# Two pieces of the column transform's last form in places of sums, and raw chunks of the hidden DFT matrices behind the forms' stores

## The chip, the cores and the metric

The kernel runs on one core of a Trainium2 chip, as one program with one launch. The metric is the device time of one execution in microseconds, the median over a few executions. A profiled execution gives a trace of every engine: PE (TensorE matmuls), PEld (its weight loads), DVE (VectorE), ACT (ScalarE), POOL (GpSimd) and SP (SyncE, which here only issues DMAs, in program order).

## What is computed

The reference takes x of 2048 rows by 640 columns and adds three things: x itself, the real part of a two-dimensional DFT of the normalised x, and a dense layer pair with GELU.

```python
xn = layernorm(x)                                # rows of 640
a = einsum("bsd,ed->bse", xn, dft_hid_re)        # wr in the kernel
b = einsum("bsd,ed->bse", xn, dft_hid_im)        # wi
y = einsum("ts,bse->bte", dft_seq_re, a) - einsum("ts,bse->bte", dft_seq_im, b)
out = x + y + (gelu(xn @ w1 + b1) @ w2 + b2)
```

All matrices are float32 and come as inputs; S is 2048, D is 640 and the hidden width F is 1536.

## The kernel before

Every product is made of three matmuls: each float32 operand is split into a high and a low part (`split`: a copy on ACT, line 157, then a subtraction on DVE, line 158), and `product` (lines 269 to 271) or `hidden` (line 287) adds high by high, high by low and low by high. One matmul is 128x128 by 128x512.

**First half: the dense layers.** Rows go through in four tiles t of 512 rows. Each has 12 steps i, one for each 128 hidden columns. In a step the program writes down `background` (loading, statistics and normalising for the next tile, ACT's square root among them), then `hidden(g + 2)` (15 matmuls), its `gelu` (line 296 on ACT, the split at 300 and 302), then `output(g)` (15 matmuls) with the `hs` of two steps before, and last, in the steps that `w_steps` lists, one step of `prep_w`. At t and step 9 the operand `XT` of the next tile is built (`prep_xt`, after `transpose_z` from `z`), and at step 10 the first `hidden` of the next tile reads it.

**The raw chunks.** `prep_w` turns wr and wi into seven matrices, kept in DRAM as `wit0` to `wit6`, for the second half's column transform. It goes over five chunks j of 128 rows, three steps k each. At k = 0 the raw chunk (`wraw0`, `wraw1`, one buffer each) is turned on DVE (`turn_w`, line 345) into `wt0` and `wt1`; before the change the next raw chunk is then asked for (`load_w`, line 340, 8 DMAs in pieces of 128 bytes). The steps then make two, two and three splits into a staging tile `wst` with two buffers, and each is stored by SP (`put_w`, line 361). A third `wst` cannot be written before the store of the first has landed. All these DMAs go through SP's one queue with the normalised rows (`xs`, line 200), `z` (line 226) and the loads of x (line 175).

**Second half: the two transforms.** The sequence transform runs in eight stages "s", one for each pair (h, t) in `blocks`; its sums u, u1, u2, v, v1, v2 lie in tiles of the pool `fr`, of which there are two sets (tags such as `u1_0` and `u1_1`). After blocks 5 and 7 follows a stage "y", the column transform of two row tiles, which the code calls hidden, too (`hidden_beside`, `hidden_entry`). A stage "y" has seven forms w of three entries each, 21 entries n. Form w multiplies sums by the five pieces of `wit[w]`, whose order is c = 0, 2, 1, 3, 4 and whose places in that order are called pos 0 to 4; piece number i is 5w + pos. `load_g(b, i)` asks for a piece. In the first stage "y" (b = 5, the one the change touches) there are five places, three in the tile `ws` and two in `gr_b`, used in turn; after each entry `hidden_entry` asks for the piece that goes into the place just read. The last form, w = 6, is 45 matmuls: its first entry (n = 18) uses pos 0 to 3 for the odd columns and pos 0 and 1 for the even ones, n = 19 uses pos 2 and 3, n = 20 uses pos 4. Of its pieces, number 30 is asked for at n = 13 and lies in a tile of its own, `gr`, that takes the place of the sum u2 of set 1; the other four use the five places.

Between the entries `hidden_beside` writes down other work of stage "y": `load_yb` reads the rows `ys` made in the first half into the places of u1 and u2 of set 0 (line 1057, runs of 256 bytes), `in_two` adds to them and stores them as output (line 803), and `load_part` reads the sums of the next block (line 786).

Of the kernel before, what the change touches and what calls it, by code (L numbers as in the profile page):

```python
# [11 lines left out]
F32R = mybir.dt.float32r  # L12
# [3 lines left out]
P = 128  # L16
Q = 4
B = 32
# [7 lines left out]
def kernel(  # L26
# [47 lines left out]
    ND = D // P  # L74
# [288 lines left out]
    def prep_w(s):  # L363

        j, k = divmod(s, 3)
        if j >= ND:
            return
        if k == 0:
            turn_w(0, j)
            turn_w(1, j)  # L370
            if j + 1 < ND:
                load_w(0, j + 1)
                load_w(1, j + 1)
        (r1, r2, r4), (i1, i2, i4) = (
            (A["wt", m][:, : 2 * P], A["wt", m][:, 2 * P : 4 * P], A["wt", m][:, 4 * P :]) for m in range(2)
        )

        if k == 0:
            put_w(0, j, r1, r4)
            put_w(1, j, i1, i4)  # L380
            add(r4, r4, i4)
        if k == 1:
            put_w(6, j, i2, i4, True)
            add(i2, i2, r2)
            put_w(2, j, i2, r4)
            add(r2, r1, r2, ALU.subtract)
            add(r1, i2, r1, ALU.subtract)
            add(i1, i1, r1, ALU.subtract)
        if k == 2:
            put_w(3, j, r1)  # L390
            put_w(4, j, i1)
            put_w(5, j, r2)

    def add(dst, a, b, op=ALU.add):
        nc.vector.tensor_tensor(dst, a, b, op=op)
# [71 lines left out]
    NW = 7  # L467
# [238 lines left out]
            form(2)  # L706


    w_steps = [(1, i) for i in (1, 2, 3, 5, 6, 7, 8)] + [(2, i) for i in (0, 1, 2, 3, 5, 6, 7, 8)]
    gelu(0, acc0)  # L710
    gelu(1, acc1)
    for g in range(NG):
        t, i = divmod(g, NF)
        if t == 0:
            prep_w1(i + 3)
            prep_w2(i + 1)
            load_w1(i + 6)
            load_w2(i + 4)
        background(t, i)
        if i == 10 and t + 1 < NT:  # L720
            load_xo(t)
        if i == NF - 1:
            acc = hidden(g + 2) if g + 2 < NG else None
            output(g)
            if acc is None:

                fourier_step(i)
                break

            def fill(k):  # L730
                for e in ((0,), (1, 2))[k]:
                    add_block(xo[t], e, oacc[t][e], f"ot{t}_{e}", bias=b2c[:, e : e + 1])

            gelu(g + 2, acc, fill)
            for e in (3, 4):
                add_block(xo[t], e, oacc[t][e], f"ot{t}_{e}", bias=b2c[:, e : e + 1])
            nc.sync.dma_start(ys[t], xo[t])
        elif i == NF - 2:
            output(g)
            if g + 2 < NG:  # L740
                gelu(g + 2, hidden(g + 2))
        else:
            acc = hidden(g + 2)
            if i == NF - 3 and t + 1 < NT:
                for j in range(ND):
                    prep_xt(t + 1, j)
                    if j + 2 < ND:
                        transpose_z(t + 1, j + 2)
            gelu(g + 2, acc)
            output(g)  # L750
        if t == 3 and i < NF - 1:
            fourier_step(i)
        if (t, i) in w_steps:
            prep_w(w_steps.index((t, i)))


    es_rows.close()
# [13 lines left out]
    def fr_tile(shape, tag, name, dtype=F32):  # L771
        return fr.tile(list(shape), dtype, tag=tag, bufs=1, name=name)
# [242 lines left out]
    def load_g(b, i):  # L1015
        if i >= NW * ND:
            return
        w, c = G[i]
        n = GWIDE[w] * P
        places = A["g", b]  # L1020
        k = i % len(places)
        if b < len(blocks) - 1 and w == NW - 1:

            k = (i - 1) % len(places)
            if c == 0:
                places, k = [fr_tile((P, 6 * P), f"u2_{sets[blocks[b]]}", f"gr_{b}", F32R)], 0
        g = places[k][:, : 2 * n].rearrange("p (a b) -> p a b", a=2)
        GT[b, i] = g
        nc.sync.dma_start(g.bitcast(F32), wits[w][c])

    def hidden_beside(b, n):


        ta, tb = blocks[b - 1][1], blocks[b][1]
        last = b == len(blocks) - 1
        x_, y_, z_ = (banks[:, k : k + 2] for k in (X, Y, Z))
        us, vs = bank(US), bank(VS)
        ya = yo[ta]

        def s(which, k):  # L1040
            return sums[(ta, tb)[which], k]

        def t2(k):
            return lambda: add(s(1, KU[k]), s(1, KV[k]), s(1, KU[k]), ALU.subtract)

        def t3(k):
            return lambda: add(s(0, KU[k]), s(1, KU[k]), s(0, KU[k]), ALU.subtract)

        def t4(k):
            return lambda: add(s(0, KV[k]), s(0, KV[k]), s(1, KU[k]), ALU.subtract)  # L1050

        def columns(k):

            return s(1 if last else 0, ("u1", "u2")[k]).rearrange("p a b -> p (a b)").rearrange("p (n e) -> p n e", n=NB)

        def load_yb(k):
            return lambda: nc.sync.dma_start(columns(k), ys[tb][:, :, 2 * k * B : 2 * (k + 1) * B])

        def copy(dst, src):
            return lambda: nc.scalar.activation(dst, src, AF.Copy)  # L1060

        def to(dst, acc, name, then=lambda: None):


            def f():
                add_turned(dst, turned(acc, name))
                then()

            return f

        def out_a(c0, c1):
            return lambda: store(ta, ya[:, :, c0:c1], c0, c1) if last else None

        def odd():
            yt = turned(us, f"yo_{tb}")
            add_turned(ya[:, :, 4 * B :], yt)
            add_turned(yo[tb, 4], yt)
            out_a(4 * B, DQ)()

        def in_two(k):  # L1080

            acc, name = s(1, ("v2", "v1")[k]), f"yb{k}_{tb}"

            def f():
                if name not in A:
                    A[name] = turned(acc, name)
                else:
                    add_turned(columns(k), A.pop(name))
                    store(tb, columns(k), 2 * k * B, 2 * (k + 1) * B, last and k == 1)

            return f

        yb1, yb2 = in_two(0), in_two(1)
        yb4 = to(yo[tb, 4], vs, f"yb4_{tb}", lambda: store(tb, yo[tb, 4], 4 * B, DQ, last))
        f5s = [lambda u=u: f5(u) for u in range(2)] if not last else [lambda: None] * 2
        f6s = [lambda u=u: f6(u) for u in range(2)] if not last else [lambda: None] * 2
        pre = {
            17: [lambda: add(s(1, "v1"), s(1, "v1"), x_)],
        }.get(n, [])
        post = {  # L1100

            0: [lambda: gather(1, tb, "v1", z_), lambda: gather(1, tb, "v", vs, op=ALU.subtract), f5s[0]],
            1: [f5s[1]],
            3: [to(ya[:, :, : 2 * B], x_, f"ya1_{ta}")],
            4: [t2(0)],
            5: [t2(1)],
            6: [to(ya[:, :, : 2 * B], y_, f"ya2_{ta}", out_a(0, 2 * B)), t2(2)],
            7: [odd],
            8: [t3(0)],
            9: [copy(s(1, "v1"), z_), t3(1)],  # L1110
            10: [t3(2)],
            11: [t4(0)],
            12: [copy(s(1, "v2"), x_), t4(1)],
            13: [load_yb(0), t4(2)],
            14: [load_yb(1), lambda: add(s(1, "v2"), s(1, "v2"), z_), yb1],
            15: [yb1],
            17: [yb2, yb2] if last else [],
            18: [yb4] if last else [yb2],
            19: [] if last else [yb2, f6s[0]],
            20: [] if last else [f6s[1], yb4],  # L1120
        }.get(n, [])
        if not last:
            if n == 13:
                post.append(lambda: load_g(b, (NW - 1) * ND))
            if n == 15:
                post.append(lambda: load_part(blocks[b + 1][1], "u1"))
            if n == 18:
                post.append(lambda: load_part(blocks[b + 1][1], "u"))
            if n == 20:
                post.append(lambda: load_a(put_off[0]))  # L1130

                def end():
                    to(ya[:, :, 2 * B : 4 * B], x_, f"ya3_{ta}")()
                    store(ta, ya, 0, DQ)

                later.append(end)
        return pre, post
# [19 lines left out]
    def hidden_entry(n, b, w, u):  # L1157
# [36 lines left out]
        for pos in mine:  # L1194
            i = w * ND + pos + len(A["g", b])
            if last or i < (NW - 1) * ND:
                load_g(b, i)
            elif i < NW * ND - 1:
                load_g(b, i + 1)

    first = 0
    for kind, what in stages:
# [67 lines left out]
```

## Time and profile before

| | us |
|---|---|
| median of 3 runs | 878.21 |
| lowest and highest | 877.09, 879.48 |
| profiled execution, its own time | 876.56 |
| span of that execution's trace | 874.8 |
| PE busy in it | 856.1 (98%) |
| DVE busy | 622.4 (71%) |
| ACT busy | 333.0 (38%) |

Times in the trace count from the start of its span; 1.76 us of the execution's time lie around the span. In a timeline a row gives start, duration, engine, line, operation, output and inputs, a count where equal ones are merged, and in brackets the idle time before it with what ended it. Matmuls overlap, so that a PE that runs without a gap starts one every 0.227 us though each is drawn 0.39 us long. A row with "SPq" is the time in which SP's queue took one DMA instruction; when the data is there is told by another view, "us to landing".

### The profile page before, as it was taken

How to read it: one execution, taken by the hardware profiler on the slowest of the kernel's cores; microseconds unless marked ns; L12 is line 12 of the kernel's file. 1: busy time of each engine (PE TensorE's matmuls, PEld its weight loads, DVE VectorE, ACT ScalarE, POOL GpSimd, SP SyncE). 2: the span in 40 equal slices, each digit the busy share in tenths (PEclk: the TensorE clock that was granted, in tenths of full speed). 3: DMA queues.
4: the chain of work that ended last, by engine and by line, in shares of the span. 5: the costliest groups of instructions: out<-in, count | busy, mean ns of one | idle time of the engine just before them, and what ended most of it. 6: DMA issues, size and time to landing. Idle time of an engine off the chain costs nothing.

```text
span 874.8 us, 10224 instructions
## 1 busy us (share of the span) xinstructions
PE 856.1 (98%) x3754; PEld 704.4 (81%) x3754; DVE 622.4 (71%) x792; ACT 333.0 (38%) x460; POOL 21.0 (2%) x22
## 2 busy tenths in 40 slices
PE   8999999999999999999999999999999699999997
PEld 6888888778888888888888888888888588888885
DVE  6554543465273678989988887889968679886586
ACT  5454433353253555434434343232323223223241
POOL 0000300030003000000000000000000000000000
PEclk9999999999999999999999999999999899999999
DMA  6746376666636984948743679574855939904465
GB/s 182 228 128 171 76 205 148 187 149 202 163 138 170 324 354 93 226 98 200 178 132 98 167 226 285 139 167 102 196 173 172 261 91 234 318 19 174 121 167 104
DMA packets 196017, 152.34 MB, mean 174 GB/s; under 512 B 70016, under 2 KB 170624, under 8 KB 194944
## 3 DMA queue, kind: packets, MB, share of 16 engines
q1 hardware_dynamic: 190016, 149.73, 63.6%
q10 hardware_dynamic: 5952, 1.97, 0.9%
q8 instruction: 29, 0.48, 0.2%
q14 instruction: 20, 0.16, 0.1%
HBM read 108.67 MB, written 42.99 MB: 173 GB/s over the span
## 4 chain that ended last, share of the span: by engine, by line
PE 87%; DVE 4%; DMA 3%; SPq 3%; ACT 1%; POOL 1%; issue 1%; DVEq 0%; ACTq 0%; POOLq 0%
PE banks L269 24%; PE banks L270 24%; PE banks L271 24%; PE banks L287 15%; DMA wit<-wst 2%; SPq L340 2%; SPq L200 1%; POOL xo L328 1%; DMA ws<-wit 1%; DVE wst L158 1%; DVE st L182 0%; DMA x<-in_A_x_dram 0%; DMA wraw<-in_A_dft_hid_im_dram 0%; DVE as L158 0%; ACT wst L157 0%
## 5 line engine op out<-in xcount | busy, mean ns | idle before, releaser
L270 PE MATMUL banks<-as,xab 128*128 128x512 f32 x407 | 158.5, 389 | 0.0
L271 PE MATMUL banks<-as,xab 128*128 128x512 f32 x407 | 158.4, 389 | 0.0
L269 PE MATMUL banks<-as,xab 128*128 128x512 f32 x407 | 158.3, 389 | 0.0
L157 ACT ACTIVATE as<-r 128x1024 fp32r<-128x1024 f32 x80 | 85.0, 1062 | 182.9 <-PE banks L271 162.2
L158 DVE TENSOR_TENSOR as<-r,as 128x1024 fp32r<-128x1024 f32 x80 | 97.1, 1215 | 49.7 <-ACT as L157 49.7
L287 PE MATMUL banks<-xt,xab 128*128 128x512 f32 x420 | 100.6, 391 | 1.6 <-DVE xt L158 1.3
L287 PEld LDWEIGHTS banks<-xt,xab 128*128 128x128 f32 x420 | 78.1, 188 | 20.3 <-DVE xt L158 3.4
L302 DVE TENSOR_TENSOR hs<-ab,hs 128x512 fp32r<-128x512 f32 x48 | 36.4, 758 | 77.7 <-ACT hs L300 77.7
L270 PEld LDWEIGHTS banks<-as,xab 128*128 128x128 f32 x407 | 76.4, 188 | 16.4 <-DVE as L158 0.4
L269 PEld LDWEIGHTS banks<-as,xab 128*128 128x128 f32 x407 | 76.4, 188 | 15.8
L271 PEld LDWEIGHTS banks<-as,xab 128*128 128x128 f32 x407 | 76.4, 188 | 15.8
L269 PE MATMUL banks<-as,xc 128*128 128x512 f32 x224 | 87.1, 389 | 0.0
L270 PE MATMUL banks<-as,xc 128*128 128x512 f32 x224 | 87.1, 389 | 0.0
L271 PE MATMUL banks<-as,xc 128*128 128x512 f32 x224 | 87.1, 389 | 0.0
L296 ACT ACTIVATE ab<-banks,b1c 128x512 f32<-128x512 f32 x48 | 33.0, 687 | 89.2 <-PE banks L287 89.1
L157 ACT ACTIVATE as<-rt 128x1024 fp32r<-128x1024 f32 x32 | 34.0, 1063 | 69.8 <-PE banks L271 57.9
L287 PE MATMUL banks<-xt,as 128*128 128x512 f32 x240 | 57.0, 389 | 0.0
L287 PEld LDWEIGHTS banks<-xt,as 128*128 128x128 f32 x240 | 45.1, 188 | 9.3
L158 DVE TENSOR_TENSOR wst<-wt,wst 128x256 fp32r<-128x256 f32 (+1 forms) x50 | 17.5, 378 | 45.4 <-ACT wst L157 45.2
L270 PEld LDWEIGHTS banks<-as,xc 128*128 128x128 f32 x224 | 42.1, 188 | 8.8
L271 PEld LDWEIGHTS banks<-as,xc 128*128 128x128 f32 x224 | 42.1, 188 | 8.7
L269 PEld LDWEIGHTS banks<-as,xc 128*128 128x128 f32 x224 | 42.1, 188 | 8.7
(161 smaller groups left out, 1397.7 us busy)
## 6 DMA issues: line engine op xcount, KB each, us to landing
raw<-in_A_dft_seq_re_dram SPq DMA_DIRECT2D x64, 256.0 KB, 5.7
raw<-in_A_dft_seq_im_dram SPq DMA_DIRECT2D x64, 256.0 KB, 5.3
wit<-wst SPq DMA_DIRECT2D x20, 384.0 KB, 2.8
ws<-wit SPq DMA_DIRECT2D x15, 384.0 KB, 5.8
xs<-x SPq DMA_DIRECT2D x64, 80.0 KB, 1.8
xo<-in_A_x_dram SPq DMA_DIRECT2D x16, 320.0 KB, 6.0
forms_ab<-xab SPq DMA_DIRECT2D x4, 1280.0 KB, 6.1
xab<-wit SPq DMA_DIRECT2D x13, 384.0 KB, 4.6
```

The source lines that it names most:

```text
L157: nc.scalar.activation(h, s, AF.Copy)
L158: nc.vector.tensor_tensor(l, s, h.bitcast(F32), op=ALU.subtract)
L200: nc.sync.dma_start(xs[c % NC * NC + k, c // NC * B : (c // NC + 1) * B], xt[c][k * B : (k + 1) * B])
L269: nc.tensor.matmul(acc, wh, mh, start=first, stop=False, skip_group_check=goes_on)
L270: nc.tensor.matmul(acc, wh, ml, start=False, stop=False, skip_group_check=goes_on)
L271: nc.tensor.matmul(acc, wl, mh, start=False, stop=last, skip_group_check=goes_on)
L287: nc.tensor.matmul(acc, W1[i][:, a, j * P : (j + 1) * P], XT[j][:, b], start=n == 0, stop=n == len(steps) - 1)
L296: nc.scalar.activation(a, acc, AF.Gelu_apprx_tanh, bias=b1c[:, i : i + 1])
L302: nc.vector.tensor_tensor(hs[:, 1], a, hs[:, 0].bitcast(F32), op=ALU.subtract)
L328: eng.tensor_tensor(d, d, yt.rearrange("p (n i) -> p n i", i=B), op=ALU.add)
L340: nc.sync.dma_start(t[q * B : (q + 1) * B], v[:, :, s0 : s0 + B])
```

## The change

Two things are changed, and no arithmetic with them.

In the first half, the next raw chunk is asked for at the end of step k = 1 of `prep_w`, after the stores of steps 0 and 1, instead of at the start of step k = 0, ahead of them. The list `w_steps` is changed with it: still 15 steps, but two of them now stand twice in one step of the tile, at (1, 3) and at (2, 5), and the steps after those come one step of the tile earlier, so that nothing stands at (1, 8) and (2, 8).

In the first stage "y", the pieces of the last form with c = 0 and c = 2 (pos 0 and 1) both get tiles of their own in places of sums of set 1, u2 as before and now u1, too. The second is asked for at n = 14. The other three go to `ws` 0, 1 and 2. The store of the first two columns of `tb`'s output (`out_b(0)`) and the loads of the next block's u1 and u are put behind all of these, at n = 18. In the last stage "y" nothing changes.

SP's order in the first stage "y" was: `ys`, piece 30, a piece of form 5, `ys`, pieces 31 and 32, the output store, the load of u1, pieces 33 and 34, the load of u. It becomes: `ys`, piece 30, a piece of form 5, `ys`, pieces 31 to 34, the output store, the loads of u1 and u.

SP's order in tile 1 was: raw chunk 1, the seven stores of chunk 0, `xs`, `z`, x, raw chunk 2, the seven stores of chunk 1. It becomes: four stores of chunk 0, raw chunk 1, three stores of chunk 0, two of chunk 1, `xs`, `z`, x, two stores of chunk 1, raw chunk 2, three stores of chunk 1, two of chunk 2.

```diff
@@ prep_w
         if k == 0:
             turn_w(0, j)
             turn_w(1, j)
-            if j + 1 < ND:
-                load_w(0, j + 1)
-                load_w(1, j + 1)
...
             add(r1, i2, r1, ALU.subtract)
             add(i1, i1, r1, ALU.subtract)
+            if j + 1 < ND:
+                load_w(0, j + 1)
+                load_w(1, j + 1)
...
-    w_steps = [(1, i) for i in (1, 2, 3, 5, 6, 7, 8)] + [(2, i) for i in (0, 1, 2, 3, 5, 6, 7, 8)]
+    w_steps = [(1, i) for i in (1, 2, 3, 3, 5, 6, 7)] + [(2, i) for i in (0, 1, 2, 3, 5, 5, 6, 7)]
...
-        if (t, i) in w_steps:
-            prep_w(w_steps.index((t, i)))
+        for k, step in enumerate(w_steps):
+            if step == (t, i):
+                prep_w(k)
@@ load_g
         if b < len(blocks) - 1 and w == NW - 1:
 
-            k = (i - 1) % len(places)
-            if c == 0:
-                places, k = [fr_tile((P, 6 * P), f"u2_{sets[blocks[b]]}", f"gr_{b}", F32R)], 0
+            k = (i - 2) % len(places)
+            if c in CHUNKS[0]:
+                k = CHUNKS[0].index(c)
+                places = {k: fr_tile((P, 6 * P), f"u{2 - k}_{sets[blocks[b]]}", f"gr{k}_{b}", F32R)}
@@ hidden_beside
                     add_turned(columns(k), A.pop(name))
-                    store(tb, columns(k), 2 * k * B, 2 * (k + 1) * B, last and k == 1)
+                    if last or k == 1:
+                        out_b(k)()
 
             return f
+
+        def out_b(k):
+            return lambda: store(tb, columns(k), 2 * k * B, 2 * (k + 1) * B, last and k == 1)
...
             if n == 13:
                 post.append(lambda: load_g(b, (NW - 1) * ND))
-            if n == 15:
-                post.append(lambda: load_part(blocks[b + 1][1], "u1"))
+            if n == 14:
+                post.append(lambda: load_g(b, (NW - 1) * ND + 1))
             if n == 18:
-                post.append(lambda: load_part(blocks[b + 1][1], "u"))
+                post += [out_b(0), *(lambda k=k: load_part(blocks[b + 1][1], k) for k in ("u1", "u"))]
@@ hidden_entry
             if last or i < (NW - 1) * ND:
                 load_g(b, i)
-            elif i < NW * ND - 1:
-                load_g(b, i + 1)
+            elif i < NW * ND - 2:
+                load_g(b, i + 2)
```

## The prediction

> **What bounds the kernel now.** I read the page first, then the waits of PE alone, then PE's timeline where it waited, then SP's queue ahead of each such place.
>
> ```profile
> span 874.8 us, 10224 instructions
> PE 856.1 (98%) x3754; PEld 704.4 (81%) x3754; DVE 622.4 (71%) x792; ACT 333.0 (38%) x460; POOL 21.0 (2%) x22
> ...
> PE banks L269 <- DMA ws<-wit: 6.5, 2, 5.1
> PE banks L287 <- DVE xt L158: 1.3, 4, 0.4
> PE banks L269 <- ACT hs L300: 1.1, 1, 1.1
> ```
>
> PE sets the time: it is busy for 98% of the span. What is left to win is its few waits. The first of these, 6.5 us in two pieces, is for a DMA that fills `ws` from `wit`: the last form of the first stage "y". The other two come from the tile change between t = 1 and t = 2, where ACT and DVE are late. The change touches just these two places. The rows of PE and then of SP's queue at the first place, with the time to landing (last number) of the second `ys` load, of piece 31 and of piece 33:
>
> ```profile
> 689.41 0.39 PE L269 MATMUL banks<-as,gr 128*128 128x512 f32 x1
> ...
> 691.66 0.50 PE L269 MATMUL banks<-as,ws 128*128 128x512 f32 x1 [1.41 <-DMA ws<-wit]
> ...
> 692.76 0.47 PE L269 MATMUL banks<-as,ws 128*128 128x512 f32 x1
> ...
> 693.30 0.40 PE L271 MATMUL banks<-as,ws 128*128 128x512 f32 x1
> 698.81 0.80 PE L269 MATMUL banks<-as,ws 128*128 128x512 f32 x1 [5.12 <-DMA ws<-wit]
> ...
> 700.26 0.63 PE L269 MATMUL banks<-as,gr 128*128 128x512 f32 x1
> 700.69 0.63 PE L270 MATMUL banks<-as,gr 128*128 128x512 f32 x1
> ...
> 708.67 0.39 PE L269 MATMUL banks<-as,xab 128*128 128x512 f32 x1
> ```
> ```profile
> 684.57 0.53 SPq L1057 DMA_DIRECT2D u<-ys  x1
> 685.20 3.30 SPq L1029 DMA_DIRECT2D ws<-wit  x2
> 689.56 2.05 SPq L803 DMA_DIRECT2D out_dram<-u  x4
> 691.65 0.95 SPq L786 DMA_DIRECT2D u<-parts  x1
> 692.70 0.39 SPq L1029 DMA_DIRECT2D ws<-wit  x1
> ...
> u<-ys SPq DMA_DIRECT2D x1, 512.0 KB, 5.5
> ws<-wit SPq DMA_DIRECT2D x1, 384.0 KB, 6.4
> ws<-wit SPq DMA_DIRECT2D x1, 384.0 KB, 6.1
> ```
>
> PE starts the form at 689.41 with piece 30 and the next stage at 708.67: 19.26 us for 45 matmuls. At full pace a matmul starts every 0.227 us (15 in 3.40 us, the chain's row further down), so 45 take 10.2 us, and 9.06 us are lost. They go so: 1.57 us until piece 31 is there (691.66 less 690.09, the end of the first three matmuls), 0.4 us until piece 32 is there, 5.28 us until piece 33 is there (698.81 less 693.53), and some 1.7 us after that, where matmuls start every 0.43 us (700.26 to 700.69). The last comes from the clock:
>
> ```profile
> 170.00:171.00 1.00, 0.09 (x1) 0.00 (x0) 1.00 (x2) 0.97 (x2) 0.00 (x0) 1.00 0.00 0
> 697.00:698.00 1.00, 0.00 (x0) 0.00 (x0) 0.00 (x0) 0.00 (x0) 0.00 (x0) 0.50 0.88 336
> 702.00:703.00 1.00, 1.00 (x6) 0.83 (x4) 0.00 (x0) 0.00 (x0) 0.00 (x0) 0.91 0.00 0
> ```
>
> The third number from the right is the granted clock: 0.50 in the long gap, back at 0.91 only in the window from 702, yet 1.00 in a gap of over one microsecond at 170. Piece 33 is late for one reason: in SP's queue it stands behind the output store, which waits for DVE until 689.56, and behind the load of u1, 512 KB.
>
> **The change in stage "y".** Piece 31 gets a place of its own and is asked for one entry earlier. That alone wins nothing: in SP's queue it still stands right behind the second `ys` load (684.57), where it stood before (685.20). Before, that instruction was held for most of the 3.30 us of the two, while `ys` drained in short runs, and it landed at 685.20 + 6.4 = 691.6, 1.5 us after `ys` (684.57 + 5.5 = 690.1). I leave it at 691.66. Piece 32 follows 1.10 us later, as now (692.76). Pieces 33 and 34 now follow at once, since their places, `ws` 1 and 2, are read for the last time in the first two entries of form 5, before 687. At the 1.10 us that parts 31 from 32, they land at 693.9 and 695.0.
>
> PE then: pos 0 until 690.09, pos 1 at 691.66, pos 2 at 692.76 until 693.5, pos 3 at 693.9 until 694.6. Piece 34 is needed only in the last entry. The other 11 products, 33 matmuls, take 7.5 us: the next stage starts at 702.0 or 702.1 instead of 708.67. The waits that are left, 1.57, 0.4 and 0.3 us, are like the one at 170, where the clock stayed at 1.00, so no slow matmuls are counted. **Gain: 6.7 us** (5.28 less some 0.3, and the 1.7 of clock).
>
> [...]
>
> What is pushed back costs nothing as far as I see. The store of two columns goes out when SP reaches it, after the pieces; nothing in the stage waits for it. The load of u1 must now wait until piece 31's place is read out, at the end of entry 18 (about 697.3), and u follows it. With the 6.1 us that a piece took beside such loads they are there by 704 to 705. The next stage reads u1 after its first form, two entries of 18 matmuls (4.08 us each): at 710. If that cover of 5 us were gone, each microsecond would cost one.
>
> **The change in tiles 1 and 2.** Here it is ACT, held by the landing of stores, that makes PE late:
>
> ```profile
> 161.37 0.42 ACT L157 ACTIVATE wst<-wt 128x256 fp32r<-128x256 f32 x1 [13.68 <-DMA wit<-wst]
> ...
> 163.34 0.67 ACT L296 ACTIVATE ab<-banks,b1c 128x512 f32<-128x512 f32 x1
> ...
> 169.84 0.67 ACT L296 ACTIVATE ab<-banks,b1c 128x512 f32<-128x512 f32 x1
> ```
> ```profile
> 169.70 0.39 PE L271 MATMUL banks<-hs,rt 128*128 128x512 f32 x1
> 171.23 0.50 PE L269 MATMUL banks<-hs,rt 128*128 128x512 f32 x1 [1.14 <-ACT hs L300]
> ...
> 179.91 5.01 PE L287 MATMUL banks<-xt,xab 128*128 128x512 f32 x20 [0.35 <-DVE xt L158]
> 184.75 0.39 PE L269 MATMUL banks<-hs,rt 128*128 128x512 f32 x1
> ```
> ```profile
> 135.33 8.95 SPq L200 DMA_DIRECT2D xs<-x  x16
> 149.87 6.20 SPq L340 DMA_DIRECT2D wraw<-in_A_dft_hid_re_dram  x4
> 158.37 12.56 SPq L361 DMA_DIRECT2D wit<-wst  x7
> ...
> wit<-wst SPq DMA_DIRECT2D x20, 384.0 KB, 2.8
> wit<-wst SPq DMA_DIRECT2D x15, 256.0 KB, 2.4
> ...
> 141.53 1.57 DVE L345 STREAM_TRANSPOSE wt<-wraw 128x640 f32<-128x640 f32 x2
> 142.40 1.34 ACT L157 ACTIVATE wst<-wt 128x256 fp32r<-128x256 f32 x4 [1.51 <-DVE wt L345]
> ```
>
> Between 169.70 and 184.75 stand 46 matmuls, 10.4 us at full pace in 15.05: 4.6 us are lost. The cause lies earlier: chunk 1's first stores stand in SP behind `xs`, `z`, x and raw chunk 2 until 158.37, so ACT waits 13.68 us for a free `wst` until 161.37, with two GELUs behind it. The second (169.84) is late for PE, and after it the `XT` of the next tile.
>
> After the change chunk 1's first two stores go out ahead of `xs`. But step (1, 3) now has a second step of `prep_w`, and ACT's square root for `xs` stands behind it: a turn (1.57) and a wait for one more store (2.4 to 2.8), about 4.2 us in all. So `xs` starts at 139.5, and the place of 149.87 in the queue comes at 154.1. There now stand the next two stores, and they drain behind `z` and x. The raw loads show when those are through: held until 149.87 + 6.20 = 156.07, which becomes 160.3. At 1.1 us each the stores land at 161.4 and 162.5; raw chunk 2, behind them, is issued by 160.3 + 2.2 + (158.37 less 156.07) = 164.8 at the latest, 163.8 if half the drain overlaps. The store behind that lands 2.4 to 2.8 us later, about 167, and ACT's last split of the chunk waits for it. Only then comes the GELU that ran at 163.34: now at 167.4, its `hs` 1.3 us later at 168.7. PE wants it at 169.93 less 3.40 = 166.5: lost 2.2 us, and 0.7 for the low part. The next GELU follows behind a turn and two splits (1.57 and 1.34) and DVE's part, near 172: lost about 1. `XT` is then in time. Sum near 4 instead of 4.6; with errors of 2 us on either side **I count 0**, bounded by a gain of 4.6 and a loss of 6 (below).
>
> ```profile
> 239.67 0.42 ACT L157 ACTIVATE wst<-wt 128x256 fp32r<-128x256 f32 x1 [11.95 <-DMA wit<-wst]
> ...
> 242.72 3.40 PE banks L287 x15
> ```
>
> In tile 2 PE loses nothing now. Behind the wait until 239.67 the change sets chunk 4's turn and two splits, one of which waits for a store (1.57, 2.4), so the GELU behind them is about 3 us later, its `hs` near 245.4. PE reads it after the 15 matmuls that end at 242.72 + 3.40 = 246.1. That is a cover of 0.7 us; I count nothing.
>
> **The rivals.** (1) *Tiles 1 and 2 are cleared.* If the stores of chunk 1 do not wait for x to drain, the GELUs are in time and 4.6 us go as well: 878.2 - 6.7 - 4.6 = 866.9. For it: two stores and a split pair now precede `xs`, and no step stands at (1, 8). Against it: the 4.2 us by which `xs` moves. (2) *The pieces are held again.* If pieces 32 and 33 are each held in the queue like 31 (3.30 us for two, nearly all of it the first), piece 33 lands some 3 us later, at 697; the gain is 3 to 4 us, 874.7. Against it: 32 was taken at once as soon as `ys` had drained. (3) *Slower, by raw loads among stores.* If raw chunk 2 behind two more stores is held 6.2 us once more (149.87), the GELU of 167.4 comes at 173.6 and PE loses some 10.2 instead of 4.6; and in tile 2 the store that chunk 4's second split waits for takes 6.2 instead of 2.4, so that `hs` comes at 249.2, 3.1 late, and 0.7 more for the low part. That is 9.4 us against 6.7 won: 880.9. It decides once that GELU comes 6.7 us later than 167.4, or 3 us later with the 3.8 of tile 2. Against it: the raw chunk is held only while x drains, which happens once. (4) *It doesn't do what it says:* u1's place is given back late (its last reader is a DVE subtraction of entry 11) and piece 31 with all behind it waits as long as piece 33 did: 878.2.
>
> **How the numbers follow.** Of the profiled execution, 876.56 us with 1.76 outside its span, 6.7 are taken: 869.9. The median of the runs is 878.21, which gives 871.5, my forecast, with 0.56. Rival 1 has 0.20, rival 2 0.12, rival 3 0.07, rival 4 0.05. About 0.3% (2.6 us) is what a measurement of this kernel can tell from no change. Faster by more: the forecast, rival 1 and nearly all of rival 2, 0.87; within: 0.06; slower: 0.07. The forecast's own errors of 2 us and rival 2 take the range up to 876.0; down it reaches to rival 1, 866.5.
>
> **What would show it.** Right: the last form of the first stage "y" lasts 12.6 us instead of 19.26, with one wait near 1.4 us at its second product, no slice of clock below 1, and in SP's queue four `wit` pieces ahead of the store. In tile 1 ACT has a wait of about 14 us for a `wit` store and PE waits at `hs` near 166.5. Wrong: a gap of over 3 us in the last form; PE waits in tile 2 for `hs` (then the cover of 0.7 us was not there); or no PE wait between 160 and 185 (then rival 1 holds).

## The result, and the profile after

| | before, us | after, us |
|---|---|---|
| median of 4 runs | 878.04 | 871.59 |
| lowest and highest | 877.09, 879.48 | 870.13, 872.75 |
| profiled execution | 876.56 | 872.75 |
| its span | 874.8 | 870.9 |

The changed kernel takes 0.9924 of the time before, with a 95% interval from 0.9902 to 0.9947: 6.4 us less by the medians, where 6.7 were forecast. The two profiled executions differ by 3.8 us only, since the one of before lies 1.5 us below its median and the one of after is the slowest of its four runs. The traces can therefore account for the 3.9 us between the two spans, not for 6.4.

The head of the page, and then the waits of PE (total, how many, longest):

```profile
span 870.9 us, 10230 instructions
...
PE 856.8 (98%) x3754; PEld 705.1 (81%) x3754; DVE 622.6 (71%) x792; ACT 332.7 (38%) x460; POOL 21.0 (2%) x22
```
```profile
PE banks L269 <- ACT hs L300: 2.7, 2, 1.8
...
PE banks L269 <- DMA gr<-wit: 1.9, 1, 1.9
PE banks L270 <- DVE hs L302: 0.7, 3, 0.2
```

The 6.5 us of waiting for `ws` are gone; 1.9 us for `gr` (piece 31 in its new place) stand there instead. The waits for `XT` behind DVE are gone as well, but those for `hs` have grown from 1.1 to 2.7 us, and the longest of them is new. PE is still the bound.

To say where time is lost, I use that PE runs the same 3754 matmuls in the same order in every kernel here. From the start of one matmul to the start of a later one I take 0.2267 us for each matmul started, which is the pace of stretches without a wait; the rest is lost. The places are named by the times of before, and in the other traces the same matmuls are taken.

| lost in, us | before | after |
|---|---|---|
| tile change t = 1 to 2 (160 to 190 us) | 4.62 | 2.46 |
| tile 2 (225 to 280 us) | 0 | 4.18 |
| first stage "y", its last two forms (665 to 712 us) | 9.15 | 3.18 |

That is 2.2 and 6.0 us won and 4.2 lost, 4.0 in all, and the spans differ by 3.9; the rest of the trace differs by 0.1.

**The last form of the first stage "y"**, PE's timeline of after, then SP's, then the time to landing of piece 31 and the median of pieces 32 to 34:

```profile
691.71 0.40 PE L269 MATMUL banks<-as,gr 128*128 128x512 f32 x1
...
694.49 0.50 PE L269 MATMUL banks<-as,gr 128*128 128x512 f32 x1 [1.91 <-DMA gr<-wit]
...
695.51 0.47 PE L269 MATMUL banks<-as,ws 128*128 128x512 f32 x1
...
696.47 0.50 PE L269 MATMUL banks<-as,ws 128*128 128x512 f32 x1
...
704.80 0.39 PE L269 MATMUL banks<-as,xab 128*128 128x512 f32 x1
```
```profile
686.93 0.53 SPq L1059 DMA_DIRECT2D u<-ys  x1
687.51 3.21 SPq L1031 DMA_DIRECT2D gr<-wit  x1
690.82 1.33 SPq L1031 DMA_DIRECT2D ws<-wit  x3
692.23 3.02 SPq L804 DMA_DIRECT2D out_dram<-u  x4
...
gr<-wit SPq DMA_DIRECT2D x1, 384.0 KB, 6.9
...
ws<-wit SPq DMA_DIRECT2D x3, 384.0 KB, 5.1
```

The form lasts 13.1 us (704.80 less 691.71) where it lasted 19.26. In SP's queue the four pieces stand ahead of the store. Piece 31 behind the second `ys` load is held 3.21 us, the three behind it go out at once, and PE takes up pieces 31, 32 and 33 at 694.49, 695.51 and 696.47.

**The tile change t = 1 to 2** in after, SP, ACT and PE:

```profile
139.40 7.33 SPq L200 DMA_DIRECT2D xs<-x  x16
...
152.29 0.95 SPq L361 DMA_DIRECT2D wit<-wst  x2
153.98 6.88 SPq L340 DMA_DIRECT2D wraw<-in_A_dft_hid_re_dram  x4
```
```profile
160.25 0.42 ACT L157 ACTIVATE wst<-wt 128x256 fp32r<-128x256 f32 x1 [12.48 <-DMA wit<-wst]
...
166.03 0.42 ACT L157 ACTIVATE wst<-wt 128x256 fp32r<-128x256 f32 x1 [4.28 <-DMA wit<-wst]
166.35 0.67 ACT L296 ACTIVATE ab<-banks,b1c 128x512 f32<-128x512 f32 x1
167.06 0.63 ACT L300 ACTIVATE hs<-ab 128x512 fp32r<-128x512 f32 x1
...
170.45 0.67 ACT L296 ACTIVATE ab<-banks,b1c 128x512 f32<-128x512 f32 x1
```
```profile
163.21 3.56 PE L287 MATMUL banks<-xt,as 128*128 128x512 f32 x15
167.74 0.49 PE L269 MATMUL banks<-hs,rt 128*128 128x512 f32 x1 [0.97 <-ACT hs L300]
168.47 0.50 PE L270 MATMUL banks<-hs,rt 128*128 128x512 f32 x1 [0.23 <-DVE hs L302]
...
172.56 0.50 PE L270 MATMUL banks<-hs,rt 128*128 128x512 f32 x1 [0.23 <-DVE hs L302]
```

ACT waits for stores to land, above all in two pieces of 12.48 and 4.28 us. The first GELU behind them (166.35) makes PE 1.1 us late and its low part 0.6 us more, the second one (170.45) costs 0.7 us, nearly all of it at the low part (172.56), and PE no longer waits for `XT`.

**Tile 2** in after: here a wait is new.

```profile
216.47 2.33 SPq L340 DMA_DIRECT2D wraw<-in_A_dft_hid_re_dram  x4
...
221.43 8.65 SPq L200 DMA_DIRECT2D xs<-x  x16
```
```profile
240.55 0.42 ACT L157 ACTIVATE wst<-wt 128x256 fp32r<-128x256 f32 x1 [14.91 <-DMA wit<-wst]
...
244.43 0.67 ACT L296 ACTIVATE ab<-banks,b1c 128x512 f32<-128x512 f32 x1
245.13 0.63 ACT L300 ACTIVATE hs<-ab 128x512 fp32r<-128x512 f32 x1
```
```profile
240.47 3.56 PE L287 MATMUL banks<-xt,as 128*128 128x512 f32 x15
245.81 0.50 PE L269 MATMUL banks<-hs,r 128*128 128x512 f32 x1 [1.78 <-ACT hs L300]
246.53 0.60 PE L270 MATMUL banks<-hs,r 128*128 128x512 f32 x1 [0.23 <-DVE hs L302]
```

The second step of `prep_w` in (2, 5) sets 3.9 us of ACT between the release at 240.55 and the GELU at 244.43. Its `hs` is ready at 245.8. PE could have read it at 240.47 + 3.40 = 243.87: 1.94 us lost, and 0.5 for the low part. Then the clock falls; the granted clock is the third number from the right:

```profile
246.00:247.00 1.00, 0.78 (x3) 0.36 (x3) 1.00 (x4) 0.60 (x2) 0.00 (x0) 0.89 0.81 326
...
250.00:251.00 1.00, 1.00 (x6) 0.83 (x5) 0.70 (x2) 0.12 (x1) 0.00 (x0) 0.90 0.31 123
```

In the three windows left out it is 0.50. What is missing from 1.00 adds up to 1.71 us of matmuls. 1.94, 0.5 and 1.71 make the 4.2.

### The profile page after: what moved, and what is told of

Its sections match the earlier page's. It is cut to its first block, busy times and chain, and to the rows that moved or that the text cites. A ratio compares the mean times of both kernels' runs of the same rounds, so it can differ in the third digit from the quotient of the medians.

```text
span 870.9 us, 10230 instructions
## 1 busy us (share of the span) xinstructions
PE 856.8 (98%) x3754; PEld 705.1 (81%) x3754; DVE 622.6 (71%) x792; ACT 332.7 (38%) x460; POOL 21.0 (2%) x22
## 4 chain that ended last, share of the span: by engine, by line
PE 81%; DMA 6%; SPq 5%; DVE 4%; ACT 2%; POOL 1%; issue 1%; DVEq 0%; ACTq 0%; POOLq 0%
PE banks L269 23%; PE banks L270 23%; PE banks L271 23%; PE banks L287 11%; SPq L340 3%; DMA wit<-wst 2%; POOL xo L328 1%; PE banks L594 1%; SPq L200 1%; DVE wst L158 1%; DMA x<-in_A_x_dram 1%; DMA gr<-wit 1%; DMA xo<-in_A_x_dram 1%; ACT wst L157 1%; DVE hs L302 1%
```

## The experiments

The theory was that of the prediction: in stage "y" the gain is that pieces 33 and 34 no longer stand behind the store and u1's load; in tiles 1 and 2 the change nets to nothing. Rivals: the tiles won something too; the new place of piece 31 is what counts; the pieces are held again.

**e1_y and e2_w: the two parts apart.** e1_y keeps the stage "y" part and has `prep_w`, `w_steps` and their loop as before; e2_w has only these new.

```diff
 # e1_y, against after
+            if j + 1 < ND:          # at k == 0 again
+                load_w(0, j + 1)
+                load_w(1, j + 1)
...
-    w_steps = [(1, i) for i in (1, 2, 3, 3, 5, 6, 7)] + [(2, i) for i in (0, 1, 2, 3, 5, 5, 6, 7)]
+    w_steps = [(1, i) for i in (1, 2, 3, 5, 6, 7, 8)] + [(2, i) for i in (0, 1, 2, 3, 5, 6, 7, 8)]
```

> Only the stage "y" part of the change; raw chunks and steps of prep_w as before. Theory (the two parts do not touch each other): the last form of the first stage "y" takes 13.1 us as in the changed kernel, PE loses 4.6 us between 169 and 185 as before and nothing in tile 2; 878.0 - 6.2 = 871.8 us. Rival (what is won in stage "y" depends on tiles 1 and 2): the last form takes another time, or the sum is off by over 2 us.

> Only the part in tiles 1 and 2: raw chunks behind the stores, two steps of prep_w at (1, 3) and at (2, 5); stage "y" as before. Theory: PE loses 2.3 us in tile 1 instead of 4.6, and in tile 2 some 2.5 us that it did not lose before, or 4.3 where the clock falls to half after that wait: between 878.2 and 880.0 us, so no gain by itself, and runs that differ by 1.8 us. Rival (tile 2's loss is a chance of one execution): 875.7 us.

Measured: e1_y 871.05 us, ratio 0.9918 [0.9898, 0.9938], beside 878.24 of before; e2_w 877.06, 0.9991 [0.9979, 1.0004], over 12 runs. So all of the gain that can be measured is that of stage "y", 7.2 us, and the part in tiles 1 and 2 by itself is not told from no change. For e2_w I had expected 878.2 to 880.0; it came out 1.1 us below that. In the trace of e1_y the loss is 5.6 us at the tile change, none in tile 2, and 3.3 in the last two forms (the last one takes 12.7 us, not 13.1); in that of e2_w it is 1.5, 1.2 and 10.2. The 5.6 stand beside 4.6 in before, with the same code there: so much one execution differs from another. The tile part of the change moves the loss within the first half, it does not leave it alone.

**e3_defer: only the order, without the new place.** Before, with the store and u1's load put behind the pieces and nothing else: piece 31 stays in `ws` 0.

```diff
 # e3_defer, against before; out_b and the store taken out of its old place, as in the change, are left out
...
-            if n == 15:
-                post.append(lambda: load_part(blocks[b + 1][1], "u1"))
             if n == 18:
-                post.append(lambda: load_part(blocks[b + 1][1], "u"))
+                post += [out_b(0), *(lambda k=k: load_part(blocks[b + 1][1], k) for k in ("u1", "u"))]
```

> Before, with one thing changed: the store of the first two columns and the load of u1 stand at entry 18, behind the last form's pieces; piece 31 stays in ws 0 as before. Theory (the gain is that pieces 33 and 34 no longer stand behind that store and load, and the place of piece 31 is worth nothing): the last form takes 13 us as with the whole change, 871.8 us, within 0.7 us of the kernel with the whole stage "y" part. Rival (the places in sums carry part of it): over 14 us in the last form, 873 to 878 us.

Measured: 871.6 us, 0.9925 [0.991, 0.994], the same as e1_y within the intervals; 3.1 us are lost in the last two forms, and the last one takes 12.85 us. The place of a sum that piece 31 was given is worth nothing that shows. Putting the store and u1's load behind pieces 33 and 34 is the whole gain; which of the two held the pieces more, no run tells apart.

**e4_ys: the second `ys` load out of the way of piece 31.** e1_y, with that load two entries later.

```diff
-            14: [load_yb(1), lambda: add(s(1, "v2"), s(1, "v2"), z_), yb1],
+            14: [*([load_yb(1)] if last else []), lambda: add(s(1, "v2"), s(1, "v2"), z_), yb1],
+            16: [] if last else [load_yb(1)],
```

> The stage "y" part, and the second load of ys moved from entry 14 to entry 16, so that pieces 31 to 34 stand ahead of it; tiles 1 and 2 as before. Theory (piece 31 lands late because it stands in the queue behind that load of 256-byte runs): the wait of about 2 us for piece 31 is gone or under 0.5 us, the last form takes 10.2 to 11 us, and the time is 2 to 2.9 us below the stage "y" part alone: 869 to 870 us. Rival (piece 31's time is set by how long any such piece takes, or by the first ys load): the wait stays at 1.5 us or more, 871.5 us.

Measured: 868.94 us, 0.9894 [0.9879, 0.9909], 2.1 us less than e1_y measured beside it, and each of its runs is below each of e1_y's. SP's timeline and landing of piece 31 (the `gr` asked for at 685.39), and PE's first and next-stage matmul:

```profile
685.39 0.43 SPq L1030 DMA_DIRECT2D gr<-wit  x1
685.92 1.61 SPq L1030 DMA_DIRECT2D ws<-wit  x3
687.62 0.53 SPq L1058 DMA_DIRECT2D u<-ys  x1
...
gr<-wit SPq DMA_DIRECT2D x1, 384.0 KB, 4.3
```
```profile
690.27 0.40 PE L269 MATMUL banks<-as,gr 128*128 128x512 f32 x1
...
700.51 0.39 PE L269 MATMUL banks<-as,xab 128*128 128x512 f32 x1
```

The same instruction that was held 3.21 us is taken in 0.43 and lands in 4.3 instead of 6.9 us. The form lasts 10.24 us, with nothing lost, and 0.6 us is lost in the form before it. What was left in stage "y" after the change was the wait behind `ys` in the queue.

**e5_t2, e6_oldsteps, e8_steps: what loses 4 us in tile 2 and wins at the tile change.** Three kernels between after and e1_y. e5_t2 is after with tile 2's steps as before; e6_oldsteps has the old steps in both tiles and the raw chunks still behind the stores; e8_steps has the new steps, and the raw chunks asked for at k = 0 as before.

```diff
 # e5_t2, against after
-    w_steps = [(1, i) for i in (1, 2, 3, 3, 5, 6, 7)] + [(2, i) for i in (0, 1, 2, 3, 5, 5, 6, 7)]
+    w_steps = [(1, i) for i in (1, 2, 3, 3, 5, 6, 7)] + [(2, i) for i in (0, 1, 2, 3, 5, 6, 7, 8)]
 # e6_oldsteps, against after
+    w_steps = [(1, i) for i in (1, 2, 3, 5, 6, 7, 8)] + [(2, i) for i in (0, 1, 2, 3, 5, 6, 7, 8)]
 # e8_steps, against after: load_w(0, j + 1) and load_w(1, j + 1) at k == 0 instead of k == 1
```

> The changed kernel with tile 2's steps of prep_w as before (none twice, the last at (2, 8)); the raw chunks stay behind the stores. Theory (the double step at (2, 5) is what costs in tile 2, since a turn and two splits with one store's landing stand ahead of a GELU that is due): PE waits for hs in tile 2 are gone (before 0, with the change 2.5 us and a half clock of 1.7), the rest stays, and the time is 1.2 to 4.3 us below the changed kernel: 868 to 870.4 us. Rival (the raw chunk behind the stores makes tile 2 late): a wait of over 1 us for hs or xt stays there, 871.6 us.

> The changed kernel with the old list of steps in both tiles; only the order of raw chunks and stores is changed there. Theory (tile 1's gain comes from the double step, which puts chunk 1's first two stores ahead of xs): PE's loss between 160 and 187 is 3 to 4.6 us, against 2.3 with the change and 4.6 to 5 before; tile 2 loses nothing; 870.5 to 871.8 us. Rival (the gain comes from the raw chunk standing behind the stores): tile 1 loses 2.3 us or less and the time is 869 us or less.

> The changed kernel with the new list of steps, but each raw chunk asked for as before, at the start of step 0, ahead of the stores. Theory (the raw chunk behind the stores is a cost in tile 1: the chunk's third step waits 4.3 us for a store queued behind it): PE loses 0 to 1 us between 160 and 187, tile 2 loses what it does with the change (1.2 to 4.3 us); 869 to 871 us. Rival (the order of loads is the gain): tile 1 loses 2.3 us or more, 871.6 us or more.

| | tile steps | raw chunks | median, us | ratio | lost: tile change | tile 2 |
|---|---|---|---|---|---|---|
| e1_y | old | early | 871.05 | 0.9918 [0.9898, 0.9938] | 5.6 | 0 |
| e6_oldsteps | old | behind stores | 872.02 | 0.9932 [0.9917, 0.9948] | 3.9 | 1.1 |
| e8_steps | new | early | 869.42 | 0.9903 [0.9886, 0.9921] | 1.7 | 0.4 |
| e5_t2 | new in tile 1 | behind stores | 870.59 | 0.9918 [0.9901, 0.9934] | 1.8 | 0.7 |
| after | new | behind stores | 871.59 | 0.9924 [0.9902, 0.9947] | 2.5 | 4.2 |
| e2_w (stage "y" as before) | new | behind stores | 877.06 | 0.9991 [0.9979, 1.0004] | 1.5 | 1.2 |

The intervals of the ratios overlap among the first five rows, so the reading rests on the traces, of which there is one each. The double step (1, 3) is what wins at the tile change: in the traces with it, e9_best's below among them, the loss is 1.5 to 2.5 us, and in those without it 3.9 to 5.6, wherever the raw chunks stand. In tile 2 PE waits long for the high part of `hs` only where two things come together. In e8_steps, with the double step (2, 5) but no raw chunk in the queue ahead of `xs`, SP, ACT and PE run like this:

```profile
218.24 8.74 SPq L200 DMA_DIRECT2D xs<-x  x16
```
```profile
237.65 0.42 ACT L157 ACTIVATE wst<-wt 128x256 fp32r<-128x256 f32 x1 [12.74 <-DMA wit<-wst]
...
241.52 0.67 ACT L296 ACTIVATE ab<-banks,b1c 128x512 f32<-128x512 f32 x1
242.22 0.63 ACT L300 ACTIVATE hs<-ab 128x512 fp32r<-128x512 f32 x1
```
```profile
243.13 0.39 PE L269 MATMUL banks<-hs,r 128*128 128x512 f32 x1
```

The same 3.9 us stand between release and GELU, but `xs` starts 3.2 us earlier than in after (218.24 against 221.43), ACT is released 2.9 us earlier, and `hs` is ready 0.3 us ahead of PE. In e5_t2, with the raw chunk ahead of `xs` and no double step, the release is late but the GELU follows it at once:

```profile
238.68 0.42 ACT L157 ACTIVATE wst<-wt 128x256 fp32r<-128x256 f32 x1 [13.70 <-DMA wit<-wst]
239.00 0.67 ACT L296 ACTIVATE ab<-banks,b1c 128x512 f32<-128x512 f32 x1
```

The raw chunk alone costs 0.7 us in e5_t2 and 1.1 in e6_oldsteps, and there PE waits for `XT`, not for `hs`. How much the two things cost together differs from one execution to the next. e2_w has the same code in both tiles as after, and its wait there is short and without a half clock:

```profile
243.39 0.49 PE L269 MATMUL banks<-hs,r 128*128 128x512 f32 x1 [0.41 <-ACT hs L300]
```

Of the four runs of after two have a granted clock of 0.996, as the profiled one among them, and two of 0.999. One stretch of 3.42 us at half clock, as in the profiled one's tile 2, is 0.002 of the span, so the fall in tile 2 is not in every execution.

Some expectations failed. For e8_steps I had expected that the double step alone would cost 1.2 to 4.3 us in tile 2; it cost 0.4. e6_oldsteps should have lost nothing in tile 2 and lost 1.1, and it and e5_t2 came out 0.2 us above their ranges. In stage "y" e8_steps loses 3.9 us, for a wait of 1.96 us with a half clock behind it.

**e9_best: what the experiments point to.** Tile 1's steps new, tile 2's old, raw chunks asked for early, the stage "y" part, and the second `ys` load as in e4_ys.

```diff
 # against after: load_w(0, j + 1) and load_w(1, j + 1) at k == 0; the second load_yb at 16 as in e4_ys
-    w_steps = [(1, i) for i in (1, 2, 3, 3, 5, 6, 7)] + [(2, i) for i in (0, 1, 2, 3, 5, 5, 6, 7)]
+    w_steps = [(1, i) for i in (1, 2, 3, 3, 5, 6, 7)] + [(2, i) for i in (0, 1, 2, 3, 5, 6, 7, 8)]
```

> Raw chunks asked for as before; tile 1's steps as in the change, tile 2's as before; the stage "y" part with the second ys load at entry 16. Theory: nothing is left of the three places where PE waited (9.1 and 4.6 us before), 878.2 - 13.7 = 864.5 us, at most 866. Rival (tile 1's gain needs the raw chunks behind the stores): 868.5 us.

Measured: 865.44 us (864.95 to 865.69), 0.9857 [0.9842, 0.9872]: 12.6 us less than before, and the interval lies below that of the changed kernel. Its windows over the three places (PE's busy time first, granted clock third from the right):

```profile
160.00:190.00 30.00, 29.11 (x125) 23.09 (x124) 17.40 (x30) 15.63 (x29) 4.65 (x4) 1.00 0.59 150
230.00:275.00 45.00, 45.00 (x200) 37.28 (x199) 22.85 (x41) 18.87 (x36) 6.75 (x5) 1.00 0.51 139
680.00:705.00 25.00, 24.68 (x110) 20.12 (x109) 20.35 (x20) 7.64 (x8) 0.00 (x0) 1.00 0.80 227
```

PE is busy throughout tile 2, 0.9 us short at the tile change and 0.3 in stage "y", at full clock: counted by matmuls, 2.0, 0 and 0.6 us are still lost, where I had expected nothing.

## Why the prediction was right, point by point

**Stage "y": right, by its own steps.** Counted from the form's first matmul, pieces 31 to 34 were forecast to be there after 2.25, 3.35, 4.5 and 5.6 us. In the trace they land after 2.7 (687.51 + 6.9 less 691.71), 3.7, 4.7 and 5.7, by the time to landing of each. The three behind 31 were taken at once; rival 2, that they are held again, does not hold. The form took 13.1 us instead of 12.6, since piece 31 was half a microsecond later than I left it: the gain in the trace is 6.0 instead of 6.7. By medians e1_y gives 7.2. That no slice of the clock fell below 1 was luck: e5_t2 and e8_steps have the same code in stage "y", and there waits of 2.07 and 1.96 us for piece 31 were followed by a half clock that cost 1.7 us (last section). A term for it was missing from the sum. That the place in a sum's tile wins nothing by itself was forecast and is shown by e3_defer. That the wait for piece 31 stays, since it still stands right behind the second `ys` load in SP's queue, was forecast too: held 3.21 us there, the piece was taken in 0.43 in e4_ys, with that load behind it. Of the store and u1's load behind the pieces, u1 was taken at 700.24 and nothing waited for it.

**The tile change: the term was mis-sized.** I had a sum near 4 us and counted no gain; 2.5 us were lost, so 2.2 were won. The step that failed is the release of the GELU: counted at 167.4, it ran at 166.35, because the two stores at 152.29 went out ahead of the queue's hold, and the hold of 6.88 us fell on the raw load behind them. The loss at `hs` was then 1.1 instead of 2.2, 0.6 instead of 0.7 for its low part, and 0.7 instead of 1 for the next.

**Tile 2: the cover of 0.7 us was not there.** The prediction named this as a sign of being wrong, and in tile 2 it was. The forecast of ACT held: GELU about 3 us later (3.9 behind the release), `hs` near 245.4 (ready at 245.76). What failed is PE's side. I took the end of its 15 matmuls, 246.1, from the trace of before. But PE comes to this place earlier by what tile 1 has won: it was through at 243.87, 2.25 us sooner. ACT's release hangs on DMAs and did not move along (240.55 against 239.67). In before's time `hs` would have been ready 0.36 us ahead of PE; so in this trace what the tile change won was lost here again, and the half clock, which I had not counted for a wait of this length, added 1.7 us.

**The sum.** The total of 871.59 us against 871.5 forecast is closer than its terms, and to that extent it is luck: in the profiled executions -6.0, -2.2 and +4.2 us stand where -6.7, 0 and 0 were forecast. The two errors in the tiles cancel in part, and e2_w shows by its median that the two tiles together come to no change that can be measured, as forecast. The profiled executions differ by 3.8 us where the medians differ by 6.4; only profiled executions leave a trace, so what the median runs of before lose beyond its profiled one is not shown. Their granted clock hints at it: it is 0.995 in the profiled one and 0.993 in the median of the 17 runs of before that stood beside e1_y, and one more stretch of 3.42 us at half clock, as in after's tile 2, would be 0.002 and cost 1.7 us.

Of the rivals, the first (866.9) came half true and was given back; the third had its place right in tile 2 but not its mechanism: no store was held behind a raw load there, `xs` was. The fourth does not hold, as piece 31 was asked for at 687.51.

## What to carry to other kernels

A load that the bound engine needs soon should not stand in a queue behind a store that waits for another engine; putting a store and a load behind such pieces was the whole gain of this change (e3_defer: 871.6 us beside 878.24), and the next thing to look at is the slow transfer just ahead of them (e4_ys: 2.1 us less than e1_y). A cover read from the trace of before holds only if the engine arrives when it did: what is won upstream can eat as much of a later cover that hangs on DMAs, as in tile 2 (PE was there 2.25 us sooner, ACT's release 0.88 us later). When a change has several parts, run them apart, for the best kernel here was the change less two parts, the raw chunks behind the stores and the double step (2, 5), with the second `ys` load moved as well.

## What the runs showed of the hardware

**Waits of about 2 us, with and without a half clock behind them.** PE kept the full clock after 1.91 us (after, stage "y") and after 2.00 us (e1_y, tile change), but not after 1.78 us (after, tile 2), 1.96 and 2.07 us (e8_steps and e5_t2, stage "y") or 2.00 us (e3_defer, tile change). Each stretch of half clock behind these four waits is 3.42 us long by the windows. That of e3_defer:

```profile
172.00:173.00 1.00, 0.90 (x2) 0.40 (x3) 0.92 (x2) 0.05 (x1) 0.00 (x0) 0.60 0.54 193
173.00:174.00 1.00, 1.00 (x3) 0.81 (x4) 1.00 (x2) 0.44 (x2) 0.00 (x0) 0.50 0.20 70
...
175.00:176.00 1.00, 1.00 (x4) 0.76 (x4) 1.00 (x4) 0.42 (x1) 0.00 (x0) 0.69 0.77 121
```

Missing from 1.00 are 0.40, 0.50, 0.50 (the window left out) and 0.31: 1.71 us of work at half pace, so 3.42 us long, as in after's tile 2. In e8_steps (0.93, three of 0.50, 0.86) and e5_t2 (0.90, three of 0.50, 0.89) 1.71 us are missing, too. The stretch around before's wait of 5.12 us in stage "y" is 6.82 us long, from 695.36 to 702.18 (0.68 in the window from 695, six of 0.50, 0.91 in that from 702). What sets the waits that lost the clock apart from those that kept it is not shown: 1.78 us lost it, 1.91 kept it, and 2.00 did both. The prediction counted no slow matmuls, by the one wait at 170 that had kept the clock at 1.00. That was too little to go by: waits of 1.78 to 2.07 us lost it.

**Piece 31 was held right behind the second `ys` load, and not ahead of it.** Right behind that load of 512 KB in runs of 256 bytes, the issue of the 384 KB piece took 3.21 us and its landing 6.9 (after); with that load behind it, 0.43 and 4.3 us (e4_ys).
